# The last 128 rows of W_down brought in by fifteen small transfers instead of one

## The chip, the cores and the metric

The kernel runs on one core of one Trainium2 chip. The metric is the device time of one execution in microseconds (us). Such a core has 16 DMA engines, and five instruction streams: TensorE (PE, with its weight loads listed apart as PEld), VectorE (DVE), ScalarE (ACT), GpSimd (POOL) and SyncE (SP). In this kernel SP issues every transfer except the load of `x`, which ACT issues.

## What is computed

One decode step of a transformer layer for 4 sequences (B = 4, one token each, D = 576). First comes attention over the last 4096 positions of a cache (32 query heads, 16 key/value heads of 128), with a residual; then a gated feed-forward layer with F = 4608, again with a residual:

```
x  = A_x
h  = x + attention(layernorm(x) @ wq, k_cache[window], v_cache[window]) @ wo
n  = layernorm(h)
g  = relu-like(n @ W_gate)          # gate * (gate > 0)
h2 = h + (g * (n @ W_up)) @ W_down  # W_down is 4608 x 576
```

All inputs and the output are bf16.

## The kernel before, in words

The kernel is a list of instructions for each engine, written out by hand, with named events. A helper class `Sched` goes over the five programs twice: once to number the events, once to emit the instructions with the semaphore waits that these numbers give. `S.dma` adds 16 to a semaphore for each transfer; the event of a transfer is the value of that semaphore when it has fully landed. `S.op` does the same for computing instructions. Nothing is reordered: each engine does its program in the order of the text.

The order of the transfers is the list `transfers`, built from top to bottom, and `prog_sync` (L248) issues them in that order: `wq` (L214, L216), the caches in pieces of 2 MB (L205 for keys, L210 for values), `wo` (L224), the pieces of `W_gate` and `W_up` (L229, L232), then `W_down` (L240). Where a transfer overwrites a part of the one large buffer `pool` that is still in use, SP waits for the last reader first. After all loads SP waits for the two result copies (`OUT0`, `OUT1`), issues the store of the output (L251) and waits for it.

`W_down` lies in `pool` as `wd_sb`, 12 groups of 3 rows of 576 values in each of the 128 partitions (`JJ = 3`, `FC = 36` chunks of 128 rows in all). The list `WD` (L235) cuts the 36 chunks into nine transfers, called wd0 to wd8 here: two of 9 chunks, five of 3 chunks, one of 2 chunks and one of a single chunk. wd8 is that last one: chunk 35, the last row of each partition, 128 rows of 576 values, 1152 bytes each. Each of the nine has a semaphore of its own.

TensorE ends the kernel with the loop over `WD`: for each transfer it waits for the landing, and then does two matmuls (128x4 against 128x288) for every chunk, 72 in all, into two accumulators. They all go through a helper, so that their line in the profile is L482. The last matmul of each accumulator is the event `DOWN0` or `DOWN1`; ACT (L342) copies the one half into `out_sb` and DVE (L475) the other, and SP stores it.

The transfers of `W_down` are described in this loop, in which a lambda makes one transfer for each entry of `WD`:

Of the kernel before, what the change touches and what calls it, by code (L numbers as in the profile page):

```python
# [13 lines left out]
D = 576  # L14
# [7 lines left out]
FC = F // 128  # L22
# [16 lines left out]
PVLAG = 5  # L39
JJ = 3  # L40
GD = 3
BIG = 1.5e38
NG = FC // JJ
HALF = F // 2
# [58 lines left out]
def bass_sequential_preLN__sliding_block_cached__glu_gated_reglu__decode_kernel(  # L103
# [12 lines left out]
    with ExitStack() as es:  # L116
# [61 lines left out]
        S = Sched()  # L178
# [3 lines left out]
        transfers = []  # L182
# [39 lines left out]
        for g in range(NWO):  # L222
            add(("wo", g), f"wo{g}", g * ROW, ROW, "ATTN",
                lambda e, o, g=g: e.dma_start(out=o.rearrange("p (q x) -> p q x", q=2),  # L224
                                              in_=A_wo[g * 1024:(g + 1) * 1024, :].rearrange("(q p e) n -> p q (e n)", q=2, e=4)))
# [8 lines left out]
        wd_sb = pool[:, 0:FC * D].rearrange("p (g x) -> p g x", g=NG)  # L234
        WD = [(0, GD * JJ), (GD * JJ, 2 * GD * JJ)] + [(g * JJ, (g + 1) * JJ) for g in range(2 * GD, NG - 1)] + [(FC - JJ, FC - 1), (FC - 1, FC)]  # L235
        for k, (f0, f1) in enumerate(WD):
            g0, j0 = divmod(f0, JJ)
            g1, nj = (f1 // JJ, JJ) if f1 - f0 >= JJ else (g0 + 1, f1 - f0)
            transfers.append((("wd", k), f"wd{k}", ["ATTN"],
                              lambda e, g0=g0, g1=g1, j0=j0, nj=nj: e.dma_start(  # L240
                                  out=wd_sb[:, g0:g1, j0 * D:(j0 + nj) * D],
                                  in_=B_W_down[g0 * 128 * JJ:g1 * 128 * JJ, :].rearrange("(g p j) n -> p g (j n)", p=128, j=JJ)[:, :, j0 * D:(j0 + nj) * D])))

        def land(name):
            return ("L",) + (name if isinstance(name, tuple) else (name,))


        def prog_sync(S):  # L248
            for name, key, free, make in transfers:
                S.dma("sync", make, key, deps=free, name=land(name))  # L250
            S.dma("sync", lambda e: e.dma_start(out=out.rearrange("b s d -> (b s) d"), in_=out_sb[:, :]), "outdma",  # L251
                  deps=["OUT0", "OUT1"], name="STORED")
            S.wait("sync", "STORED")
# [91 lines left out]
        def prog_dve(S):  # L345
# [17 lines left out]
            for x in range(2):  # L363
# [3 lines left out]
                                              axis=AX.X, op=ALU.add), name="M0")  # L367
            S.op(v, lambda e: e.tensor_scalar(out=mask[:, 1, :], in0=mask[:, 0, :], scalar1=2 * BIG, scalar2=-BIG, op0=ALU.mult, op1=ALU.add),
                 deps=["M0"], name="M1")
            S.op(v, lambda e: e.tensor_scalar(out=mask[:, 2, :], in0=mask[:, 0, :], scalar1=-2 * BIG, scalar2=BIG, op0=ALU.mult, op1=ALU.add),  # L370
                 name="M2")
# [106 lines left out]
        def prog_pe(S):  # L478
# [133 lines left out]
            for k, (f0, f1) in enumerate(WD):  # L612
                deps = [land(("wd", k))] + (["D_HHT"] if k == 0 else [])
                for f in range(f0, f1):
                    g, j = divmod(f, JJ)
                    for u in range(2):
# [3 lines left out]
                        deps = []  # L620

        progs = [("gpsimd", prog_pool), ("sync", prog_sync), ("scalar", prog_act), ("vector", prog_dve), ("tensor", prog_pe)]
        S.begin(False)
        for _, p in progs:
# [33 lines left out]
```

## Time and profile before

| what | value |
|---|---|
| time, median of 3 executions | 384.68 us (384.5 to 385.1) |
| the profiled execution's own time | 385.3 us |
| its span, first to last instruction | 383.5 us |
| mean granted TensorE clock in it | 0.907 |
| busy share: PE / DVE / ACT / POOL | 75% / 52% / 13% / 2% |
| read from memory in the span | 159.58 MB, 416 GB/s |
| queue of SP's loads, share of the 16 DMA engines | 98.6% |

The profile is of one execution, taken by the hardware's profiler. "Busy" is time within instructions of an engine. The page's strip of 40 slices gives busy tenths for each engine and for the 16 DMA engines together, and the clock that the throttle granted to TensorE. The table by stage gives the same for chosen stretches of the span. The chain of waits goes back from the last instruction to whatever released it. The list of DMA issues gives the duration of the issuing instruction on SP and the time from issue to landing. Under these views lie the trace's single records: the start of every instruction, every step of a DMA semaphore, and the start and duration of every packet that a DMA engine moved.

### The profile page before, as it was taken

To read this page: it belongs to the slowest core of one execution; us is meant where nothing else is said; L and a number is where in the kernel's file an instruction comes from. 1 tells how busy PE (TensorE), PEld (TensorE's weight loads), DVE (VectorE), ACT (ScalarE), POOL (GpSimd) and SP (SyncE) were. 2 spreads that over 40 slices of the span, in tenths; PEclk is the share of its full clock that TensorE was granted. 3 is DMA by queue.
4 is the path that set the end of the run, shared out by engine and by line. 5 is a ranking of instruction groups with operands and counts; after the bars stand their busy time and mean duration, and the time that the engine had idled before them with its cause. 6 is when DMAs were issued, how large, how long until landed. Compare 5 with 4: busy or idle time off the path is not lost.

```text
span 383.5 us, 4157 instructions
## 1 busy us (share of the span) xinstructions
PE 288.7 (75%) x1827; PEld 130.2 (34%) x1842; DVE 198.8 (52%) x181; ACT 51.5 (13%) x125; POOL 7.9 (2%) x20
## 2 busy tenths in 40 slices
PE   0059649976996699679958994899499788874387
PEld 0053213322432243224322431343134233374355
DVE  0259789269437854774486558645855450011000
ACT  4021040021102110311030004100400021100000
POOL 4000000000000000000000000000000000000000
PEclk9999958998999899989998999899989998955559
DMA  7999999999999999999999999999999999999994
GB/s 316 426 424 426 431 424 432 426 424 431 426 424 434 424 427 431 426 427 431 426 427 434 424 424 434 427 424 432 427 424 434 426 423 434 403 417 424 414 415 172
DMA packets 14306, 159.86 MB, mean 417 GB/s; under 512 B 1480, under 2 KB 1616, under 8 KB 4560
## 3 DMA queue, kind: packets, MB, share of 16 engines
q1 hardware_dynamic: 14280, 159.59, 98.6%
q8 instruction: 14, 0.23, 0.2%
q10 hardware_dynamic: 8, 0.00, 0.0%
q14 instruction: 4, 0.03, 0.0%
HBM read 159.58 MB, written 0.00 MB: 416 GB/s over the span
## 4 chain that ended last, share of the span: by engine, by line
PE 41%; DMA 23%; issue 15%; DVE 14%; ACT 5%; POOL 1%; SPq 0%; POOLq 0%
PE sc L482 23%; PE pb L482 18%; DMA pool<-in_A_k_cache_dram 9%; DMA pool<-in_B_W_down_dram 7%; DMA pool<-in_A_wo_dram 7%; ACT P L323 4%; DVE kT L394 4%; DVE probT L413 4%; DVE rmx L397 4%; POOL bcm L274 1%; DVE bias L409 0%; DVE rowsum L418 0%; DVE t L405 0%; DVE pmax L400 0%; DVE bmin L407 0%
## 5 line engine op out<-in xcount | busy, mean ns | idle before, releaser
L394 DVE STREAM_TRANSPOSE kT<-pool 128x2048 f32<-128x2048 f32 x64 | 144.5, 2291 | 54.6 <-DMA pool<-in_A_k_cache_dram 49.4
L482 PE MATMUL sc<-kT,qz 128*128 128x512 bf16 x497 | 131.9, 418 | 51.2 <-DVE kT L394 47.6
L482 PE MATMUL pb<-pool,prob 128*16 128x512 bf16 x512 | 116.4, 386 | 0.8 <-DMA pool<-in_A_v_cache_dram 0.8
L482 PEld LDWEIGHTS sc<-kT,qz 128*128 128x128 bf16 x512 | 49.0, 102 | 130.9 <-DVE kT L394 57.0
L482 PEld LDWEIGHTS pb<-pool,prob 128*16 128x16 bf16 x512 | 43.5, 91 | 71.0 <-issue 15.3
L323 ACT ACTIVATE P<-sc,bias 128x512 f32<-128x512 f32 x32 | 22.2, 714 | 176.5 <-DVE bias L409 176.5
L397 DVE TENSOR_REDUCE rmx<-sc 128x2 f32<-128x2048 f32 x8 | 18.3, 2292 | 34.0 <-PE sc L482 34.0
L413 DVE STREAM_TRANSPOSE probT<-P 128x2048 f32<-128x2048 f32 x8 | 18.5, 2311 | 7.8 <-ACT P L323 7.8
L482 PE MATMUL pb<-hnT,pool 128*128 128x4 bf16 x288 | 8.8, 167 | 9.8 <-DMA pool<-in_B_W_up_dram 5.0
L489 PE MATMUL pb<-ident_b,xn_bf 4*128 4x4 bf16 (+1 forms) x5 | 0.4, 175 | 20.3 <-ACT xn_bf L287 20.3
L308 ACT COPY cp<-pb 128x512 f32<-128x512 f32 x8 | 4.7, 584 | 67.5 <-PE pb L482 67.5
L482 PEld LDWEIGHTS pb<-hnT,pool 128*128 128x128 bf16 x288 | 8.2, 104 | 10.3 <-DMA pool<-in_B_W_up_dram 5.2
L422 DVE RECIPROCAL rs_sb<-pb 128x32 f32<-128x32 f32 x4 | 1.4, 338 | 19.8 <-PE pb L482 19.8
L482 PE MATMUL pb<-selT,cp 128*128 128x16 f32 x64 | 7.9, 255 | 4.3 <-ACT cp L308 4.3
L473 DVE TENSOR_TENSOR hhT<-pb,gate_sb 128x144 bf16<-128x144 f32 x1 | 0.3, 308 | 20.9 <-ACT gate_sb L339 20.9
L330 ACT CAST prob<-probT 128x1024 bf16<-128x1024 f32 x8 | 8.4, 1044 | 19.0 <-DVE rs L416 19.0
L482 PE MATMUL pb<-pool,hhT 128*4 128x288 bf16 x72 | 10.5, 315 | 0.4 <-DMA pool<-in_B_W_down_dram 0.4
L482 PEld LDWEIGHTS pb<-selT,cp 128*128 128x128 f32 x64 | 8.2, 191 | 6.3 <-ACT cp L308 5.3
L274 POOL PARTITION_ALL_REDUCE bcm<-pmax x8 | 3.1, 386 | 290.6 <-DVE pmax L400 290.6
L301 ACT COPY qz<-qrep 32x64 bf16<-32x64 bf16 x32 | 7.8, 245 | 7.3 <-DVE qrep L431 7.0
L482 PEld LDWEIGHTS pb<-pool,hhT 128*4 128x4 bf16 x72 | 6.6, 93 | 4.3 <-DMA pool<-in_B_W_down_dram 0.7
L489 PEld LDWEIGHTS pb<-ident_b,xn_bf 4*128 4x128 bf16 (+1 forms) x5 | 0.3, 108 | 20.3 <-ACT xn_bf L287 20.3
(94 smaller groups left out, 71.5 us busy)
## 6 DMA issues: line engine op xcount, KB each, us to landing
pool<-in_A_k_cache_dram SPq DMA_DIRECT2D x32, 2048.0 KB, 28.1
pool<-in_A_v_cache_dram SPq DMA_DIRECT2D x32, 2048.0 KB, 26.1
pool<-in_A_wo_dram SPq DMA_DIRECT2D x4, 1152.0 KB, 21.7
pool<-in_B_W_gate_dram SPq DMA_DIRECT2D x4, 1152.0 KB, 25.7
pool<-in_B_W_up_dram SPq DMA_DIRECT2D x4, 1152.0 KB, 24.5
pool<-in_A_wq_dram SPq DMA_DIRECT2D x4, 1024.0 KB, 7.9
pool<-in_B_W_down_dram SPq DMA_DIRECT2D x2, 1296.0 KB, 27.2
pool<-in_B_W_down_dram SPq DMA_DIRECT2D x5, 432.0 KB, 14.5
```

What stands on the lines that cost most here:

```text
L274: S.op(g, lambda e, n=n: e.partition_all_reduce(bcm[:, n % 2, :], pmax[:, n % 2, :], 128, bass_isa.ReduceOp.max), deps=deps, name=("PAR", n))
L301: S.op(a, lambda e, src=src, dst=dst: e.copy(out=dst, in_=src), deps=deps, name=("QZ", n) if g == 3 else None, signal=g == 3)
L308: S.op(a, lambda e: e.copy(out=cp[:, n % 2, :], in_=pb[PVB + n % 2]), deps=deps, name=("CP", n))
L323: S.op(a, lambda e, n=n, th=th, u=u: e.activation(out=P[:, th * 1024 + u:(th + 1) * 1024:2], in_=sc[:, th * 1024 + u:(th + 1) * 1024:2], f ...
L330: S.op(a, lambda e, n=n: e.copy(out=prob[:, n % 2, :, :, :], in_=probT[:, :, 0:NHB].rearrange("p t (r x) -> p r t x", x=4)), deps=deps, na ...
L394: S.op(v, lambda e: e.transpose(out=dst, in_=src), deps=deps, name=("TR", i))
L397: S.op(v, lambda e: e.tensor_reduce(out=rmx[:, n % 2, :], in_=sc[:, :].rearrange("p (x u) -> p u x", u=2), axis=AX.X, op=ALU.max), deps=[( ...
L413: S.op(v, lambda e: e.transpose(out=probT[:, :, :].rearrange("p t j -> p (t j)"), in_=P[:, :]), deps=[("EXP", n, 1)] + ([("CMP", n - 1)] i ...
L422: S.op(v, lambda e: e.reciprocal(out=rs_sb[:, b, :], in_=pb[OB][:, 64 + b * H:64 + (b + 1) * H]), deps=[("SUM", b)], name=("RS", b))
L473: S.op(v, lambda e: e.tensor_tensor(out=hhT[:, :, :], in0=pb[GUB][:, FC * B:2 * FC * B].rearrange("p (f b) -> p f b", b=B), in1=gate_sb[:, ...
L482: S.op(t, lambda e: e.matmul(o, lhsT=l, rhs=r, start=start, stop=stop, skip_group_check=skip), deps=deps, name=name, signal=name is not None)
L489: S.op(t, lambda e, c=c, w=w, src=src, base=base: e.transpose(out=tpv[0:w, base + c * 4:base + (c + 1) * 4], in_=src[0:B, c * 128:c * 128 ...
```

## The change

For the entry of `WD` that ends at `FC` (wd8), the one transfer of 128 partitions is replaced by fifteen transfers. They take 15, 14, 13, 12, 11, 10, 9, 9, 8, 7, 6, 5, 4, 3 and 2 partitions, 128 together, in that order; the bytes and their places stay the same. All fifteen add to the same semaphore `wd8`, 16 each; only the last has a name, so that TensorE waits for 240 instead of 16. The other eight transfers, the matmuls and the programs of the other engines are the same.

```diff
+LAST = (15, 14, 13, 12, 11, 10, 9, 9, 8, 7, 6, 5, 4, 3, 2)
...
         for k, (f0, f1) in enumerate(WD):
             g0, j0 = divmod(f0, JJ)
             g1, nj = (f1 // JJ, JJ) if f1 - f0 >= JJ else (g0 + 1, f1 - f0)
+            if f1 == FC:
+                p0 = 0
+                for n in LAST:
+                    transfers.append((("wd", k) if p0 + n == 128 else None, f"wd{k}", ["ATTN"],
+                                      lambda e, g0=g0, j0=j0, p0=p0, n=n: e.dma_start(
+                                          out=wd_sb[p0:p0 + n, g0, j0 * D:(j0 + 1) * D],
+                                          in_=B_W_down[(g0 * 128 + p0) * JJ:(g0 * 128 + p0 + n) * JJ, :].rearrange("(p j) n -> p j n", j=JJ)[:, j0, :])))
+                    p0 += n
+                continue
             transfers.append((("wd", k), f"wd{k}", ["ATTN"],
...
         def prog_sync(S):
             for name, key, free, make in transfers:
-                S.dma("sync", make, key, deps=free, name=land(name))
+                S.dma("sync", make, key, deps=free, name=land(name) if name else None)
```

## The prediction

> **What bounds the kernel now.** I read the page's strip first: the DMA engines stand at 9 tenths from the second slice to the last but one. Up to the end the kernel is a stream of loads. The change lies behind all of it, so only the end matters. The second view is the chain of waits, from 366 us on:
>
> ```profile
> 343.77 26.88 DMA pool<-in_B_W_down_dram
> 370.64 0.04 issue
> 370.69 10.55 PE pb L482 x72
> 381.24 0.02 issue
> 381.26 0.45 DVE out_sb L475
> ```
>
> The reader is to see that the chain leaves the DMA at 370.64, when wd0, the first piece of W_down, has landed. From there all 72 matmuls run as one piece of 10.55 us with no wait inside it. The time line of the same stretch says so too: one idle time ahead of the 72, none between them. Its last lines:
>
> ```profile
> 380.69 0.21 PEld L482 LDWEIGHTS pb<-pool,hhT 128*4 128x4 bf16 x2
> 381.14 0.39 ACT L342 CAST out_sb<-pb 4x288 bf16<-4x288 f32 x1 [12.64 <-PE pb L482]
> 381.26 0.45 DVE L475 CAST out_sb<-pb 4x288 bf16<-4x288 f32 x1 [12.42 <-PE pb L482]
> 381.80 0.34 SPq L251 DMA_DIRECT2D out_dram<-out_sb  x1
> ```
>
> The two weight loads at 380.69 are those of wd8: TensorE comes to the wait for it at 380.69. The list of DMA issues tells when wd8 is there:
>
> ```profile
> pool<-in_B_W_down_dram SPq DMA_DIRECT2D x1, 144.0 KB, 12.2
> ```
>
> It is issued at 367.95 (trace), so it lands at 367.95 + 12.2 = 380.13, which is **0.56 us before TensorE asks for it**. The other transfers are early too: wd1 to wd7 land 0.4 to 1.7 us ahead of their matmuls (semaphore records). The table by stage shows the same from the side of the DMA:
>
> ```profile
> 375.00:376.00 1.00, 1.00 (x10) 0.70 (x9) 0.00 (x0) 0.00 (x0) 0.00 (x0) 1.00 1.02 408
> 376.00:377.00 1.00, 1.00 (x10) 0.68 (x9) 0.00 (x0) 0.00 (x0) 0.00 (x0) 1.00 0.84 333
> 377.00:378.00 1.00, 1.00 (x11) 0.68 (x8) 0.00 (x0) 0.00 (x0) 0.00 (x0) 1.00 0.61 242
> 378.00:379.00 1.00, 1.00 (x11) 0.70 (x9) 0.00 (x0) 0.00 (x0) 0.00 (x0) 1.00 0.44 169
> 379.00:380.00 1.00, 1.00 (x11) 0.70 (x9) 0.00 (x0) 0.00 (x0) 0.00 (x0) 1.00 0.15 52
> 380.00:381.00 1.00, 1.00 (x10) 0.64 (x8) 0.00 (x0) 0.00 (x0) 0.00 (x0) 1.00 0.00 0
> ```
>
> The second column is PE's busy time, the last two the share of the 16 DMA engines and GB/s. The DMA engines run dry one after another: the sixteen steps of wd8's semaphore go from 376.52 to 380.13, 3.6 us apart. PE meanwhile never pauses. The end is TensorE's, counted from wd0.
>
> **The change part by part.**
>
> *Bytes on the engines.* The packet records give the price of a row: in wd8 one engine's eight packets of 1152 bytes start 47 ns apart, the semaphore's packet starts 47 ns after the last, and the next transfer's data 6 to 7 ns later. So eight rows and an increment take 8 x 47 + 7 = 383 ns, and a row with an increment of its own 54 ns. How are n rows spread? The store of 4 rows shows four packets side by side (starts 382.58 to 382.71) and a semaphore that moves in 5 steps, against 16 for a load of 128 rows. I take it that n rows go to n engines, one each. If these are always the same first n, the sixteen engines get 15, 15, 14, 13, 12, 11, 10, 9, 8, 6, 5, 4, 3, 2, 1 and 0 rows instead of 8 each: the fullest engine ends 15 x 54 - 383 = 427 ns later, the empty one 383 ns earlier.
>
> Which engines lag is not in the records, so I bound it. If the full ones are those that end first now, wd8's landing goes from 380.13 to 379.61 (the engine that lands at 379.94 now, with one row: 379.94 + 0.05 - 0.38). If they are those that end last, it goes to 380.13 + 0.43 = 380.56. Both lie before 380.69. **Taken: 0 us.** TensorE's own run hides either; in the worse case 0.13 us of cover is left.
>
> The Trainium skill, "DMA: Bandwidth & Descriptors", section "Why a DMA increments its semaphore by 16 and not by 1", says that a load from SP uses the largest number of engines up to 16 that divides the row counts of both sides, and the lowest-numbered ones. By that rule n rows do use n engines and the loads above hold; the 5 steps of the 4-row store agree, and no record here names an engine. By the rule the sum stays 0.
>
> *Instructions on SP.* One issue goes and fifteen come, all after 367.95. Behind them on SP stands only the output store, which has to wait for DVE until 381.7. Nothing on SP's queue is passed. The nearest rows for one issue, each from the view of its own line:
>
> ```profile
> L240 SPq DMA_DIRECT2D pool<-in_B_W_down_dram x3: 892/1008/2405, 364.6 to 367.9; - x3
> ```
>
> ```profile
> L251 SPq DMA_DIRECT2D out_dram<-out_sb x1: 337/337/337, 381.8 to 381.8; - x1
> ```
>
> ```profile
> L205 SPq DMA_DIRECT2D pool<-in_A_k_cache_dram x32: 535/606/1187, 4.0 to 265.4; - x32
> ```
>
> The first (the transfers of the same place, minimum, median and maximum in ns) are issues into full queues: some 12 us of loads stand ahead of them, and they go at the pace at which the engines drain. The second is the only small transfer of SP, 4 rows into empty queues. The third is 128 rows into queues that are not full. Between issues lie some 45 ns. Lower end 0.34 + 0.05 = 0.39 us each, upper end 1.01 + 0.05 = 1.05 us. The limit: the store lands 1.31 us after its issue (381.80 to 383.11), so the fifteenth issue must start by 380.69 - 1.31 = 379.38, which is (379.38 - 367.95) / 14 = **0.82 us** per issue. I take 0.39 to 0.65 us (the second and third rows), because what fills a queue is rows: a 128-row transfer adds 8 and an increment to each engine, these add at most 1 and an increment. Where the old ones had to wait for 9 entries to drain (some 1.2 us at 24 rows and one increment of wd1 in 3.16 us), these wait for 2, some 0.25 us. The fifteenth issue then starts at 373.4 to 377.1 and its rows stand in the queue before the engines come to them. **Taken: 0 us.**
>
> *TensorE.* The same 72 matmuls; one wait with another value. 0 us.
>
> **The sum** is 0 against the profiled execution's 385.3 us (span 383.5 and 1.8 around it). The median of the three executions is 0.6 lower, 384.68, and nothing moves it: 384.7.
>
> **The rivals.**
>
> *Slower: the issues are the bound.* If an issue costs what the blocked row says whatever its size, the fifteenth starts at 367.95 + 14 x 0.94 = 381.1 to 367.95 + 14 x 1.05 = 382.65, lands 1.31 later at 382.4 to 384.0, and the two last matmuls start then instead of 380.69: +1.7 to +3.3 us, 386.4 to 388.0. It decides from 0.82 us per issue on. For it: they are the nearest rows in place. Against it: every issue into queues with room took 0.34 to 0.70 us.
>
> *Slower: the small transfers go one behind the other on an engine.* If each increment had to land before the next row moves, an engine with 15 rows would take 15 x (0.05 + 0.38) = 6.4 us, where 0.38 is the time from the last semaphore packet (379.75) to its landing (380.13). That is 6.0 us more: 382.5 on the earliest engine, 386.1 on the latest, so 386.5 to 390.1. The same size comes out if odd row counts all fell on one engine (128 x 54 ns = 6.9 us). Against it: wd7 and wd8 land 0.36 us apart on the same engine, no more than the 383 ns of data. The Trainium skill speaks against the change here: the same page, "Rules for kernel authors", wants small transfers merged, since below 64 KB one pays mostly overhead; these have 2 to 17 KB. Its "Anatomy of one DMA" estimates the fixed part at about 2.0 us on the GpSimd path; fifteen of these in a row would be 30 us, and by that the end would come some 18 us later. That they overlap is what the 0.36 us above shows for two transfers of 128 rows; for single rows no run here shows it.
>
> *Faster: the landing is the bound where no profiler runs.* If the timed executions got the full clock sooner (the first 12 of the 72 matmuls run at a granted 0.50, 240 ns apart instead of 122), TensorE would wait for wd8, and the earlier landing would bring up to 0.52 us, 0.13%. Only a gain of the clock as well would make more of it, and nothing in the change reaches the clock.
>
> **How the numbers follow.** A difference of 0.2%, 0.8 us, is about what a measurement of this kernel can tell from no change. Hidden (both ends of the landing, and the small gain just named): 0.67, at 384.7, with its own range 384.0 to 385.4. Issues bound: 0.17. One behind the other: 0.08. Faster by more than 0.2%: 0.08. The range goes from 384.0 to 388.0, the upper end of the issues; what is left out is the faster case and most of the serial one. Faster 0.08, same 0.67, slower 0.25.
>
> **What would show it.** Right: the 72 matmuls in one piece of some 10.5 us, wd8's last step before 380.7, fifteen issues of 0.35 to 0.65 us done by 378. Wrong: an idle time of TensorE ahead of the last two matmuls with the DMA as releaser; fifteen issues of 0.9 us or more; 1152-byte packets of one engine further apart than 60 ns; or 72 matmuls that start at another time, which I have no reason for.

## The result: 1.6 us slower

| | before | changed |
|---|---|---|
| median of the executions | 384.83 us (384.5 to 385.1, 4) | 386.39 us (386.32 to 386.79, 4) |
| ratio | | 1.0044, 95% interval 1.0033 to 1.0056 |
| the profiled execution: time, span | 385.3, 383.5 us | 386.79, 385.0 us |

The time lies in the range that the prediction gave (384.0 to 388.0), but its likeliest case, no change, did not come; that 386.4 is inside is luck, since that part of the range stood for another mechanism. The profile after, first the time line of the end:

```profile
370.62 9.18 PEld L492 LDWEIGHTS pb<-pool,hhT 128*4 128x4 bf16 x66 [0.75 <-DMA pool<-in_B_W_down_dram]
370.62 10.01 PE L492 MATMUL pb<-pool,hhT 128*4 128x288 bf16 x70 [0.46 <-DMA pool<-in_B_W_down_dram]
379.98 0.33 PEld L492 LDWEIGHTS pb<-pool,hhT 128*4 128x4 bf16 x4 [0.18 <-DMA pool<-in_B_W_down_dram]
382.35 0.09 PEld L492 LDWEIGHTS pb<-pool,hhT 128*4 128x4 bf16 x2 [2.04 <-DMA pool<-in_B_W_down_dram]
382.35 0.41 PE L492 MATMUL pb<-pool,hhT 128*4 128x288 bf16 x2 [1.72 <-DMA pool<-in_B_W_down_dram]
```

The piece of 72 matmuls is now one of 70 and one of 2, and between them TensorE waits 1.72 us for a transfer of W_down. That pause is the whole difference: the 70th matmul still starts 0.35 us earlier than in the first profile (380.34 against 380.69). The view of the issuing lines says whether SP was late with it:

```profile
L244 SPq DMA_DIRECT2D pool<-in_B_W_down_dram x15: 253/315/1088, 367.8 to 373.6; - x15
```

It was not: the first issue took 1.09 us, about as long as the one of before (1.01), the other fourteen took 0.25 to 0.37 us, and the last began at 373.6, almost 6 us before the limit of 379.38. Then the chain of waits and, from the table by stage, three stretches:

```profile
373.62 8.69 DMA pool<-in_B_W_down_dram
382.31 0.04 issue
382.35 0.42 PE pb L492 x2
```

```profile
379.00:380.00 1.00, 1.00 (x11) 0.57 (x9) 0.00 (x0) 0.00 (x0) 0.00 (x0) 1.00 0.12 38
380.00:381.00 1.00, 0.63 (x5) 0.23 (x4) 0.00 (x0) 0.00 (x0) 0.00 (x0) 1.00 0.00 0
381.00:382.00 1.00, 0.00 (x0) 0.00 (x0) 0.00 (x0) 0.00 (x0) 0.00 (x0) 1.00 0.00 0
```

The two say something odd together. The DMA engines stop moving packets at 380.05 (next to last column: 0.00 from 380 on), and yet the transfer is there only at 382.31. The bytes are not late; the semaphore is. The semaphore's records show how: the last five steps of wd8's semaphore come at 381.58, 381.76, 381.94, 382.12 and 382.31, 0.18 us apart, while the packets of these increments left their engine 53 ns apart, the last at 380.05. wd7's last step was at 379.93. Between it and 382.31 lie 2.38 us, 13 x 0.183, and the engine whose packets end last moves 13 rows of wd8, each followed by an increment of its own (one run of packets, 53 ns apart, from 379.35 to 380.05).

### The profile page after: what moved, and what is told of

It is laid out like the page before. It is cut to its first block, busy times and chain, and to the rows that moved or that the text cites. A ratio compares the mean times of both kernels' runs of the same rounds, so it can differ in the third digit from the quotient of the medians.

```text
span 385.0 us, 4171 instructions
## 1 busy us (share of the span) xinstructions
PE 289.6 (75%) x1827; PEld 130.6 (34%) x1842; DVE 198.6 (52%) x181; ACT 51.5 (13%) x125; POOL 7.9 (2%) x20
## 4 chain that ended last, share of the span: by engine, by line
PE 35%; DMA 20%; DVE 16%; issue 16%; SPq 7%; ACT 5%; POOL 1%; POOLq 0%
DMA pool<-in_A_k_cache_dram 18%; PE sc L492 18%; PE pb L492 17%; DVE kT L404 7%; SPq L250 6%; ACT P L333 4%; DVE probT L423 3%; DVE rmx L407 3%; DMA pool<-in_B_W_down_dram 2%; SPq L244 1%; POOL bcm L284 1%; DVE bias L419 0%; ACT cp L318 0%; ACT prob L340 0%; ACT qz L311 0%
```

## The theories, and what the runs said

*Theory 1*: the increments of one DMA engine land one behind the other, at least 0.18 us apart; a row with an increment of its own costs 0.18 us, not the 0.054 of its packets. *Theory 2*: the load is uneven, or it is the rows and their bytes. *Theory 3*: 128 increments of one semaphore stand in each other's way. *Theory 4*: fifteen issues or transfers cost time as such, wherever they stand. The differences below are medians of executions of the kernel and of the one before on the same chip.

### Even load, eight increments for each engine

```diff
-LAST = (15, 14, 13, 12, 11, 10, 9, 9, 8, 7, 6, 5, 4, 3, 2)
+LAST = (16,) * 8
```

> wd8 goes in eight transfers of 16 rows: every engine gets 8 rows, as before, but 8 increments instead of 1, 128 in all as in the changed kernel. Theory 1 (each engine's increments land one behind the other, 0.18 us apart): wd8's last step 8 x 0.18 = 1.4 us after wd7's, near 381.3; TensorE pauses some 0.6 us ahead of the last two matmuls; +0.5 to +0.7 us on before. Theory 2 (the uneven load of the engines is what lands late): the load is even again, last step near 380.2, +0. Theory 3 (128 increments of one semaphore stand in each other's way): last step near 382.3, +1.6 us as in the changed kernel. Theory 4 (the number of issues on SP): eight issues end earlier, +0.

Measured 385.68 us against 384.64 (ratio 1.0020, 1.0007 to 1.0033). wd8's last step came at 381.23, 1.36 us or 8 x 0.17 after wd7's (379.87). The end of its time line:

```profile
381.27 0.09 PEld L492 LDWEIGHTS pb<-pool,hhT 128*4 128x4 bf16 x2 [0.71 <-DMA pool<-in_B_W_down_dram]
381.28 0.41 PE L492 MATMUL pb<-pool,hhT 128*4 128x288 bf16 x2 [0.40 <-DMA pool<-in_B_W_down_dram]
```

The pause stands at the same place and is shorter. The load is even here, so theory 2 in its first form falls; there are 128 increments on one semaphore as in the changed kernel, and theory 3 wanted its 382.3. The place of the landing is theory 1's; the time is 1.04 us over before instead of 0.5 to 0.7. What is missing in that sum comes below.

### A semaphore for each of the fifteen

```diff
-                for n in LAST:
-                    transfers.append((("wd", k) if p0 + n == 128 else None, f"wd{k}", ["ATTN"],
+                for i, n in enumerate(LAST):
+                    transfers.append((("wd", k, i), f"wd{k}_{i}", ["ATTN"],
...
+                if f1 == FC:
+                    deps = [land(("wd", k, i)) for i in range(len(LAST))]
```

> The fifteen transfers as in the changed kernel, but each with a semaphore of its own; TensorE waits for all fifteen. Theory 1 (the order is kept within an engine, whatever the semaphore): last step near 382.3, steps of one engine 0.18 us apart, +1.6 us on before. Theory 3 (one semaphore is the bottleneck): last step near 380.2 to 380.6, +0 to +0.2 us.

Measured 387.02 us against 384.64 (1.0049, 1.0032 to 1.0066):

```profile
382.36 0.56 PE L492 MATMUL pb<-pool,hhT 128*4 128x288 bf16 x2 [1.87 <-DMA pool<-in_B_W_down_dram]
```

Theory 3 is out. With fifteen semaphores every step can be told. The latest steps of the transfers of 15, 14, 13, 12 and 11 rows are 379.95, 380.14, 380.31, 380.48 and 380.65, a chain 0.17 to 0.19 us apart that ends there. From the transfer of 10 rows on the latest steps are those of another chain, 380.74, 380.93 and so on, which ends with the transfer of 4 rows at 382.02 (wd7's last step: 379.77). All other steps form such chains too, 0.16 to 0.21 us apart, and with each shorter transfer one chain ends. So n rows do lie on n engines, the same first ones each time, as the prediction took it, and the chain that ends last is that of the fourth engine, with 13 increments. Nor do the increments of different engines stand in each other's way: from 380.93 on this chain's steps are almost alone, and they come no closer together. The time is 0.8 us over theory 1's +1.6, though the last step came earlier than the 382.3 expected. A part of it is that TensorE's weight load comes 0.31 us after the last landing, against 0.04 in the changed kernel; fifteen waits instead of one stand ahead of it.

### Fewer increments, about as many rows

```diff
+LAST = (30, 26, 22, 18, 14, 10, 6, 2)
```

> wd8 goes in transfers of 30, 26, 22, 18, 14, 10, 6 and 2 rows: if n rows are spread evenly over the largest number of engines up to 16 that divides n, an engine that had 13 rows with 13 increments has 11 rows with 7 increments. Theory 1 (increments): last step 7 x 0.18 = 1.3 us after wd7's, near 381.2, +0.4 to +0.6 us on before. Theory 2 in the form that it is the rows (0.18 us for each row): 11 x 0.18 = 2.0 us, near 381.9, +1.2 us.

Measured 385.42 us against 384.64 (1.0015, 1.0003 to 1.0026):

```profile
381.14 0.41 PE L492 MATMUL pb<-pool,hhT 128*4 128x288 bf16 x2 [0.72 <-DMA pool<-in_B_W_down_dram]
```

Last step 381.10, 1.41 us after wd7's (379.69): 7 increments of 0.20, if it is again the fourth engine that ends last. For 11 rows of 0.18 it would have been 1.98. The increments count here, not the rows: one for each transfer that the engine takes part in. The time is again above what theory 1 said, +0.8 instead of 0.4 to 0.6.

### Increments without the rows

The kernel before, and behind its single wd8 the fifteen shapes as transfers of 64 bytes a row into a buffer that nobody reads. wd8 has no name then; TensorE waits until all sixteen have landed, which add to one semaphore:

```diff
...
+        scr = sb("scr", [16, 15 * 32], BF16)
+        for i, n in enumerate(LAST):
+            transfers.append((("wd", len(WD) - 1) if i == len(LAST) - 1 else None, f"wd{len(WD) - 1}", [],
+                              lambda e, n=n, i=i: e.dma_start(out=scr[0:n, i * 32:(i + 1) * 32], in_=B_W_down[0:n, 0:32])))
```

> The kernel before, with wd8 as one transfer of 128 rows; behind it fifteen transfers of 15 down to 2 rows of 64 bytes each, which go to a buffer that nobody reads and add to wd8's semaphore, so that TensorE waits for them too. Theory 1: it is the increments, whatever bytes they carry: last step 13 to 15 x 0.18 = 2.3 to 2.7 us after 380.1, near 382.4 to 382.8, pause of 1.7 to 2.1 us, +1.6 to +2.1 us on before. If the cost is in the 1152 bytes of each row: last step near 380.3 to 380.6, +0.

Measured 386.21 us against 384.59 (1.0038, 1.0025 to 1.0052), as much as the change itself. The last two matmuls in its time line:

```profile
381.85 0.41 PE L488 MATMUL pb<-pool,hhT 128*4 128x288 bf16 x2 [1.58 <-DMA scr<-in_B_W_down_dram]
```

All 128 rows of W_down came in one transfer; what TensorE waits for 1.58 us are 64-byte rows with an increment each. The last step was at 381.81, earlier than the 382.4 to 382.8 expected; which engine it was is not known (steps 0.20 us apart lead up to it, 381.21, 381.41, 381.61, among those of other engines). Theory 2's second form, the bytes, is out.

### Four increments for each engine

```diff
+LAST = (32,) * 4
```

> wd8 goes in four transfers of 32 rows: every engine has 8 rows and 4 increments. Theory 1 (increments of one engine land 0.18 us apart): last step 4 x 0.18 = 0.73 us after wd7's, near 380.6, just ahead of TensorE's wait at 380.7: no pause over 0.1 us ahead of the last two matmuls, 0 to +0.1 us on before. A cost per transfer, whatever lies in it, would have to be seen here too: 4 of 15 of the changed kernel's 1.6 us, +0.4.

Measured 385.21 us against 384.59 (1.0020, 1.0002 to 1.0038):

```profile
380.91 0.09 PEld L492 LDWEIGHTS pb<-pool,hhT 128*4 128x4 bf16 x2 [0.30 <-DMA pool<-in_B_W_down_dram]
```

Theory 1 said 0 to 0.1, and 0.6 came. The +0.4 of a cost for each transfer as such, theory 4, lies within the interval (0.1 to 1.5 us): 0.1 us a transfer would also give the 0.8 and 1.0 of eight and the 1.6 of fifteen, so these times alone do not decide against it. The landing was almost where it was expected (last steps 380.39, 380.55, 380.71, 380.86, 0.16 us apart; wd7's, 380.24, was 0.3 to 0.7 later than in the other profiles). What was wrong is the other side of the comparison: that TensorE comes to wd8 at 380.7 in the kernel before.

### The kernel before, twice more

> The kernel before, unchanged, profiled once more. Its first profiled execution took 385.3 us, 0.7 more than the median of the others. If the time before is set by wd8's landing in most executions, this one has a span near 382.8 us, the full clock granted earlier than 373.4, wd8's last step near 380.1 and the last two matmuls right behind it, with a pause of TensorE in front of them or in front of those of wd6 or wd7. If TensorE's own run sets it in every execution, the 72 matmuls are in one piece of 10.5 us again and the span is near 383.5.

> As the run ahead of it: a third look at the kernel before, for how much the clock's return and the landing vary between executions.

They took 385.11 and 384.75 us, spans 383.3 and 382.9. In the first the 72 matmuls are one piece of 10.40 us again, and TensorE comes to wd8 at 380.52, 0.38 us after its landing. The second, which is near the median of 384.64:

```profile
371.76 8.90 PE L482 MATMUL pb<-pool,hhT 128*4 128x288 bf16 x67
372.00 6.85 PEld L482 LDWEIGHTS pb<-pool,hhT 128*4 128x4 bf16 x53
379.03 1.31 PEld L482 LDWEIGHTS pb<-pool,hhT 128*4 128x4 bf16 x12 [0.17 <-DMA pool<-in_B_W_down_dram]
380.57 0.39 ACT L342 CAST out_sb<-pb 4x288 bf16<-4x288 f32 x1 [12.18 <-PE pb L482]
```

Here a wait has entered the piece (at 379.03, for wd6), and TensorE comes to wd8 at 380.13, 0.07 us after its landing at 380.06. There is almost no cover. The clock's records tell why the three profiles differ. In all of them the first matmul on W_down begins at 370.6 to 370.7 at half the clock; the full clock comes back at 373.9 in the first profile, at 373.6 in the second and at 372.8 in the third. Each microsecond of that costs TensorE half a microsecond of work (its matmuls are 240 ns apart at half the clock and 122 at the full one). wd8's landing stays at 380.06 to 380.14 in all three. The 0.56 us of the prediction were those of an execution whose clock came back late; of 21 executions of before on one chip, 14 had a span of 382.6 to 382.9 us, and the first profile's 383.5 lies in the tail above them.

With that the sums close. Measured against the landing of wd8 in the kernel before, 380.1:

| kernel | increments on the engine that ends last | wd8's last step | later than 380.1 | measured, us |
|---|---|---|---|---|
| four of 32 | 4 | 380.86 | 0.8 | +0.6 |
| eight transfers, 30 to 2 rows | 7 | 381.10 | 1.0 | +0.8 |
| eight of 16 | 8 | 381.23 | 1.1 | +1.0 |
| single wd8 and 64-byte rows | not told | 381.81 | 1.7 | +1.6 |
| fifteen with the early residual (below) | not told | 381.60 | 1.5 | +1.6 |
| fifteen (the change) | 13 | 382.31 | 2.2 | +1.6 |
| fifteen, a semaphore each | 13 | 382.02 | 1.9 | +2.4 |

All but the last two agree within some 0.2 us. The profiled execution of the change was itself the longest of four, 0.4 us above the median. In the kernel with fifteen semaphores TensorE started later after the landing, by 0.27 us; the rest, some 0.2 us, is open.

### The fifteen issued earlier

Ahead of wd3:

```diff
+        tail = transfers[-len(LAST):]
+        del transfers[-len(LAST):]
+        transfers[-5:-5] = tail
```

> The fifteen transfers of the changed kernel are issued ahead of wd3 instead of behind wd7; TensorE's order is the same. Theory 1: the increments that lag are made up for while the data of wd3 to wd7 moves (1.05 us for each increment), so wd7's last step is near 380.1 to 380.5, and no pause is longer than 0.3 us: 0 to +0.35 us on before. Theory 4 (the fifteen issues or transfers cost time wherever they stand): +1.6 us.

Ahead of wd0 (`transfers[-len(WD) + 1:-len(WD) + 1] = tail`):

> The fifteen transfers of the changed kernel are issued ahead of wd0, so that all of W_down's other data follows them on the engines; TensorE's order is the same. Theory 1: the lag of the increments is made up while wd0's 24 rows per engine move (3.2 us); what is left is the heavier load of the engine that ends last, some 0.3 us: TensorE's 72 matmuls in one piece again, from near 371.0 on, +0.2 to +0.5 us on before. Theory 4 (fifteen more transfers cost time wherever they stand): +1.6 us.

Measured 386.21 against 384.64 (1.0035, 1.0022 to 1.0047), and 387.35 against 384.59 (1.0065, 1.0048 to 1.0083). Here theory 1, in the form that I gave it, falls: the lag is not made up while data moves. Theory 4's +1.6 came true in the first; the second is worse than the change. The time line of the second:

```profile
369.89 0.09 PEld L496 LDWEIGHTS pb<-ident_f,R_sb 64*4 64x4 f32 x2 [0.43 <-issue]
372.22 10.42 PEld L496 LDWEIGHTS pb<-pool,hhT 128*4 128x4 bf16 x72 [2.24 <-DMA pool<-in_B_W_down_dram]
372.22 10.74 PE L496 MATMUL pb<-pool,hhT 128*4 128x288 bf16 x72 [1.96 <-DMA pool<-in_B_W_down_dram]
```

TensorE starts 1.5 us later, because wd0's last step comes at 372.18 (380.1 for wd8 in before has become 381.32 for wd7 here). Fifteen engines were there at 370.90; one was 1.3 us behind, and stayed so through wd7 (380.02 and 381.32). From 372.22 on TensorE then runs in one piece. To see where an engine loses that time, the first of the two was profiled again:

> The fifteen transfers issued ahead of wd3, as before in this study, profiled again: the first profile's 385.6 us was at the low end of its executions (median 386.2). If a row with an increment of its own holds its engine for 0.18 us also where data follows, the packets of wd3 and later on the loaded engines are stretched, and wd7's last step moves to 381 or later in an execution of 386.2 us, by as much as the time is longer. If the data is not held up, the extra 0.6 us are somewhere else, ahead of wd3.

It took 386.55 us. One engine of sixteen is behind from wd3 on: second to last and last steps are 376.26 and 377.57 for wd3, 380.12 and 381.53 for wd7. This decides against theory 4: a cost of the transfers as such would be expected on all engines, and fifteen of them are done at 380.12, where the kernel before is done at 380.13. The late engine seems to be the fourth again: the fifteen transfers' last step, 377.39, is 2.37 us or 13 x 0.18 after the last of wd2, which goes ahead of them, and in the run with the fifteen ahead of wd0 the same distance is 2.34 us. The packets say how: between 371.9 and 375.7 some 30 of those of 3456 bytes take 0.35 to 0.6 us instead of 0.135 (two in each profile of the kernel before, 0.37 us), and four of 1152 bytes 0.15 to 0.19 us instead of 0.05. The changed kernel shows the start of the same: packets of 1152 bytes run 53 ns apart at first, and five near 378 take 0.09 to 0.18 us. So, as far as the packets tell, the increments hold their engine: some packets can run ahead of them, then the data waits for the pace of 0.18 us. Theory 1 has to read: **a row with an increment of its own costs its engine up to 0.18 us, wherever it stands in the queue**; at the end of the queue one sees it as a late semaphore, ahead of data as long packets. Why the pace is 0.18 us, and how many packets run ahead, was not tried. Nor was it separated whether it is the increment that costs this or something else that a transfer does once on each of its engines.

```profile
373.87 3.10 PE L496 MATMUL pb<-pool,hhT 128*4 128x288 bf16 x24 [0.41 <-DMA pool<-in_B_W_down_dram]
377.61 0.90 PE L496 MATMUL pb<-pool,hhT 128*4 128x288 bf16 x6 [0.64 <-DMA pool<-in_B_W_down_dram]
380.87 1.63 PE L496 MATMUL pb<-pool,hhT 128*4 128x288 bf16 x12 [0.16 <-DMA pool<-in_B_W_down_dram]
```

This is that run's time line: one long wait (for wd1, 0.41), another for wd3 (0.64), and then a small one for each piece, since TensorE follows the one late engine to the end.

### TensorE's own run taken out of the way

The twelve small matmuls that add the residual are moved ahead of the gate and up matmuls, and the first two pieces of W_down are cut into three each (`GD = 1`), so that TensorE can start at 368.8:

> A version to beat both: the kernel before, wd8 as one transfer; the twelve small matmuls that add the residual are done ahead of the gate and up matmuls instead of behind them, and W_down comes in eleven pieces of three chunks, one of two and one of one, so that TensorE starts on it some 1.8 us earlier. By theory 1 wd8's last step stays near 380.1 and becomes what TensorE waits for: the last two matmuls start near 380.2 instead of 380.7, -0.4 to -0.7 us on before. Rival: TensorE is held up by something else between 369 and 380, no change.

Measured 384.64 against 384.59 us (0.9995, 0.9986 to 1.0004): no gain. The end of its time line:

```profile
378.01 2.64 PE L482 MATMUL pb<-pool,hhT 128*4 128x288 bf16 x18 [0.22 <-DMA pool<-in_B_W_down_dram]
379.02 1.31 PEld L482 LDWEIGHTS pb<-pool,hhT 128*4 128x4 bf16 x12 [0.43 <-DMA pool<-in_B_W_down_dram]
380.57 0.39 ACT L342 CAST out_sb<-pb 4x288 bf16<-4x288 f32 x1 [12.25 <-PE pb L482]
```

TensorE waits for each piece now, and its result is out at 380.57, as in the kernel before of 384.75 us. The landing of the pieces was the bound already. What the edit did bring is that the tail is gone: its 11 executions lie between 384.45 and 384.75, the 21 of before between 384.42 and 385.70. The same with the fifteen transfers:

> The kernel with the early residual and small first pieces, and wd8 in the fifteen transfers of the change: nothing of TensorE's own run is left to hide the landing. If in the timed executions the landing is the bound before and after, this is as slow as the changed kernel, +1.6 to +1.9 us on before. If TensorE's run still hid a part, it would be under the changed kernel's time by 0.3 us or more.

Measured 386.21 against 384.64 (1.0045, 1.0028 to 1.0063), as slow as the changed kernel (1.0044):

```profile
381.64 0.41 PE L492 MATMUL pb<-pool,hhT 128*4 128x288 bf16 x2 [1.03 <-DMA pool<-in_B_W_down_dram]
```

So none of the change's cost is hidden behind TensorE in the timed executions, and a faster kernel would have to end the loads earlier. With one increment for each transfer there is little to win: emptying the latest engines of wd8 altogether would bring at most the 0.36 us that wd8 takes there (379.77 to 380.13), less than any slowdown measured here, and TensorE, which came to wd8 only 0.07 us after its landing in the execution of 384.75 us, could use little of it. No run tried it.

## Why the prediction was right and wrong, step by step

- *What bounds the kernel*: wrong for most executions. The step "0.56 us before TensorE asks for it" is true of the profiled execution and was carried to all. The table had the sign of it: that execution's 385.3 us was 0.6 above the median, and the granted clock of 0.50 in the first 12 matmuls, which the prediction named under its third rival, was the reason (in the execution of 384.75 us it was some 9). The landing as the bound, which is that rival's mechanism, was thus the usual case, not the exception; its gain did not come, because the landing moved later and not earlier.
- *Bytes on the engines*: the step "a row with an increment of its own 54 ns" failed. The packets at the end kept to it (53 ns); the landings took 0.16 to 0.21 us. The bounds on wd8's landing, 379.61 to 380.56, missed 382.31 by 1.75 us because a packet's start was taken for the price of its landing. That n rows use the same first n engines was right, and the rule of the Trainium skill, "DMA: Bandwidth & Descriptors", section "Why a DMA increments its semaphore by 16 and not by 1", agrees with it.
- *Instructions on SP*: right that they cost nothing. The fourteen issues after the first took 0.25 to 0.37 us, even less than the 0.39 to 0.65 taken with the gap of 0.05; the limit of 0.82 was never near. The first rival, for which the range went up to 388.0, gave the measured time, 386.4, but by a mechanism that did not occur. That the time lies in the range is therefore luck.
- *The second rival, one increment behind the other on an engine*: this is what happened, at 0.18 us a row instead of the 0.43 that it was given. The reason held against it, wd7 and wd8 landing 0.36 us apart, was no evidence: eight rows of 47 ns take longer than one increment of 0.18, so it is hidden there. It got a chance of 0.08, and most of its times were left out of the range.
- The rule of the Trainium skill that was weighed against the change, to merge small transfers ("Rules for kernel authors"), came out as it says. Another section of that page, "Anatomy of one DMA", says for the GpSimd path that the gap which a semaphore's write leaves is about one cycle, and that the write is in effect free. For these loads, which SP issues, the trace shows a gap of 6 ns between packets, but the runs show 0.16 us at least between landings; what an increment costs here is decided by that.

## What to carry to other kernels

Count increments for each DMA engine, not only rows and bytes: here a transfer has to give each of its engines about 0.18 us of data (four rows of 1152 bytes) for its increment to be free (an estimate from 47 ns a row: eight rows hid it, two did not, four were not tried), and cutting the last transfer finer than that makes it land later, or holds up what follows. Read a landing from the semaphore's steps and not from the last packet; DMA engines that are idle while a wait on DMA goes on are the sign. And before a slack of half a microsecond is used as cover, look at more than one execution, or at least ask why the profiled one is above the median.

## What I had not expected of the hardware

- Increments of one engine land 0.16 to 0.21 us apart when each follows one or two rows, whether the rows have 1152 or 64 bytes and whether they share a semaphore; the packets of these rows run 53 ns apart until some dozen increments are outstanding (in the changed kernel the last packet left at 380.05, 2.26 us or twelve steps before its landing), and some that come later on a loaded engine take 0.09 to 0.19 us.
- The sixteen engines end the same stream 3.6 to 4.3 us apart (wd7's steps, in the profiles in which no small transfer stands ahead of it), and not in the order in which small transfers fill them. Counted in that order, the first three and the fifth to seventh landed wd7 between 377.1 and 378.3 in the run with fifteen semaphores, the eighth, ninth and sixteenth first (375.9, 375.9, 376.5), the fourth and the tenth to fifteenth last (379.4 to 379.8). Loads that fall from the first engine to the last therefore put 13 increments on one of the latest.
- A small transfer is cheaper to issue than a large one: 253 ns for 2 rows to 365 ns for 12 in the changed kernel, against 414 to 435 for most transfers of 16 to 128 rows at the same place whose issue did not have to wait (one took 366 ns).
- The full clock came back at 371.3 to 375.9 in the fourteen profiles of this study. Between three executions of the kernel before it differed by 1.1 us (372.8 to 373.9), which moved its span by up to 0.6 us (382.9 to 383.5).
